# A spectral filter and a gated feed-forward in one kernel: the first block's filter sums, weight conversions, GpSimd sums and two copies are moved

## The chip, the cores and the metric

The kernel runs on one core of one Trainium2 chip. The metric is the device time of one execution in microseconds (us); lower is better. Each engine of the core (TensorE, here PE; VectorE, DVE; ScalarE, ACT; GpSimd, POOL; SyncE, SP) works through its own instructions in the order in which the program issues them, and waits on semaphores for the others. Transfers are issued by SP, ACT or POOL and run on 16 DMA engines.

## The reference

```python
# x: (8, 3008, 256); filt_r, filt_i: (1505, 256); w_in: (256, 2048); w_out: (2048, 256)
X = np.fft.rfft(x, axis=1)
y = np.fft.irfft(X * (filt_r + 1j * filt_i)[None], n=3008, axis=1)   # a filter along the sequence
t = y.reshape(24064, 256)
h = t @ w_in
g = h * np.clip(h + 3.0, 0.0, 6.0) / 6.0
out = g @ w_out
```

Everything is float32 in the result. The kernel may be handed weights whose words the program has to reassemble (`w_conv` below), so each piece of `w_in` and `w_out` passes through a "conversion" before it can be used.

## The kernel before, in words

**The two halves.** The first half turns each of the 8 batches into its spectrum, multiplies by the filter and turns it back. The length 3008 is split as 47 times 64, so the transform is a product with small tables (`a_unit`, L385), a second product (`b_unit`), the filter (`f_unit`, L449 to L451, and its sums in `y_unit`, L459 and L460), a first product back (`bi_unit`, L471 with its copies L474) and a last one (`n_unit`, L524), which writes the tokens into a ring in SBUF (`xn`). Between these steps the data goes through DRAM: `z_store` and `t2_load`, `g_store` and `t4_load`.

The second half takes 512 tokens at a time (a "block", 47 of them) and for each block walks through 8 pieces `p` of the hidden dimension, 256 wide each. One (block, piece) pair is a **step**; steps are numbered 0, 1, 2, ... over all blocks. Block 0 (steps 0 to 7) uses plain products: `plain_up(p)` (L657, 8 instructions on PE), `relu` on ACT (L615), `hswish` on DVE (L620), and one step later `plain_down(p)` (L668, 16 instructions). From block 1 on, a Strassen-like scheme with 7 instead of 8 products is used (`up_1` to `up_5`, L570; `down`, L646). It needs sums of quarter matrices: of the tokens (`t_sums`, POOL, L563), and of the weights (`w_sums`, POOL, L299), the latter made once for all blocks.

**Conversions.** The 16 weight pieces, `w_in[0]`, `w_out[0]`, `w_in[1]`, ..., `w_out[7]`, are numbered 0 to 15. Number i is loaded by SP (`w_load`, L260), has its absolute value taken by ACT (`w_abs`, L266) and is finished by seven DVE instructions (L275, L277, L279, L281, L288, L290, L293), which write it into `w_all`. The staging buffers are few, so the load of a later piece is issued only behind the conversion that frees its buffer; the read that frees it is L288. Numbers 0 to 3 are converted before step 0 ends its first products; the other 12 are put into the steps by a list. Converted piece 2p is needed by `plain_up(p)` at step p, piece 2p+1 by `plain_down(p)` at step p+1.

**Order.** [...] `at(step, fn, ...)` puts a piece of work of the first half, of the conversions or of the sums into a step. In a step of block 0 the order is `plain_up(p)`, then the work put there that PE should meet early (`a_unit`, `b_unit`, `bi_unit`, `n_unit`), then `plain_down(p-1)`, then the rest in the order in which it was put there. An engine's instruction that has to wait holds up all that the program put behind it on that engine.

**Buffers that the change touches.** `rp` has two buffers, used by `relu` and, in batch 0, also for the two results of `y_unit` (i = 10 and 11, made just before step 0). Their last readers are the matmuls of `bi_unit(0, 10)` at step 0, which the program issues behind `plain_up(0)`; the two `relu` of step 0 therefore wait for them. `t1p` has two buffers too. Batch 0 uses them for the results of `bi_unit(0, 0)`, `(0, 4)` and `(0, 8)` on their way to DRAM; from step 2 on, `a_unit` of batch 1 uses them. The PSUM banks of `plain_up` (`al`, `be`) are single: the products of step p+1 wait until `hswish` of step p has read them.

**Batch 1.** Its `a_unit(1, c)`, c = 0 to 7, lies in steps 2 to 9, one a step. Each has two 128x512 results in PSUM, which ACT copies to SBUF (L388), and four stores on SP (`z_store`, L402).

Of the kernel before, what the change touches and what calls it, by code (L numbers as in the profile page):

```python
# [10 lines left out]
FP32 = mybir.dt.float32  # L11
# [20 lines left out]
P = 128  # L32
D = 256
# [5 lines left out]
NB = HC // XC  # L39
# [6 lines left out]
NP = DFF // 256  # L46
# [90 lines left out]
def kernel(  # L137
# [9 lines left out]
    nc = tc.nc  # L147
# [15 lines left out]
    def pool(name, bufs, **kw):  # L163
        return ctx.enter_context(tc.tile_pool(name=name, bufs=bufs, **kw))

    const = pool("const", 1)
    t1p = pool("t1p", 2)
    t2p = pool("t2p", TB)
    sp = pool("sp", 2)
    yp = pool("yp", 3)  # L170
    t3p = pool("t3p", T3B)
    xtp = pool("xtp", 2)
    rp = pool("rp", 2)
# [21 lines left out]
    st = {}  # L195
# [173 lines left out]
    def bank(b):  # L369
        if b:  # L370
            return psF.tile([P, 512], FP32, name="psf", tag="f")
        st["bank"] = i = (st.get("bank", -1) + 1) % 4
        return psO.tile([P, 2, 2, P], FP32, name="po%d" % i).rearrange("p a u m -> p (a u m)")
# [4 lines left out]
    def a_unit(b, c):  # L378
        xc = xs[:, (b * NB + c) % 3, :, :]
        t = t1p.tile([P, XC // 2, 2, D], FP32, name="t1")  # L380
        ps = [bank(b).rearrange("p (j d) -> p j d", d=D) for h in range(2)]
        for j in range(2):
            for g in range(2):
                for h in range(2):
                    nc.tensor.matmul(ps[h][ts(g, 64), j, :], wa[ds(h * 64, NA), ds((c * XC + 2 * g + j) * 2 * KH, 64)],  # L385
                                     xc[ds(h * 64, NA), 2 * g + j, :], start=True, stop=True)
        for h in range(2 if b == 1 else 1):
            nc.scalar.activation(out=t[:, :, h, :], in_=ps[h], func=AXT.Copy)  # L388
        st["t1", b, c] = t, ps[1]


    def a_sums(b, c):
        t, ps = st["t1", b, c]
        nc.vector.tensor_tensor(out=t[:, :, 1, :], in0=t[:, :, 0, :], in1=ps, op=ALU.subtract)
        nc.vector.tensor_tensor(out=t[:, :, 0, :], in0=t[:, :, 0, :], in1=ps, op=ALU.add)  # L395

# [56 lines left out]

    def y_unit(b, i):
        s1, s2 = st["y", b, i]
        y = yp.tile([P, 2, D], FP32, name="y") if b else rp.tile([P, 512], FP32, name="r", tag="r").rearrange(
            "p (u d) -> p u d", u=2)
        re, im = slice(0, HALF), slice(HALF, P)
        nc.vector.tensor_tensor(out=y[re], in0=s1[re], in1=s1[im], op=ALU.subtract)  # L459
        nc.vector.tensor_tensor(out=y[im], in0=s2[re], in1=s2[im], op=ALU.add)  # L460
        st["y", b, i] = y
# [34 lines left out]
    for b in range(B):  # L496
        j = 0
        while j < HC:
            n = 1 if b == 0 and j == NJ else min(NJ, HC - j)
# [229 lines left out]


    EARLY = (a_unit, b_unit, bi_unit, n_unit)

    def at(step, fn, *a):
        plan.setdefault((step, fn in EARLY), []).append((fn, a))

    with tc.manual_schedule():
# [38 lines left out]
        ps = psU.tile([P, 512], FP32, name="al")  # L775
# [27 lines left out]
        for c in range(NT):  # L803
            for i in (2 * c, 2 * c + 1):
                b_unit(0, i)
                f_unit(0, i)
                if c == NT - 1:
                    y_unit(0, i)
            if c + 1 < NT:
                turn(c + 1)  # L810
            if c:
                bi_unit(0, 2 * c - 2)
                (g0_first if c == NT - 1 else lambda i: g_store(0, i))(2 * c - 2)
            if c == 4:
                t4_load(0, 0, KH - 3 * TC, 1)
# [20 lines left out]
        at(0, bi_unit, 0, NU - 2)  # L836
        at(0, g_store, 0, NU - 2)

        for i, s in enumerate((0, 1, 1, 2, 2, 3, 3, 4, 4, 5, 5, 6)):
            at(s, convert_one)  # L840
        for p in range(NP):
            for i in range(2):
                for late in range(2):
                    at(p + 6, w_sums, 2 * p + i, late)

        at(0, wai_load)
        at(2, x_load, 1, 2)
# [31 lines left out]
        def places(n):  # L879
            if n == 1:  # L880
                return (list(range(2, NB + 2)), [12, 13, 15, 18, 19, 20, 22, 23, 26, 27, 28, 30],
                        [14, 15, 16, 19, 21, 22, 24, 25, 27, 29, 30, 31], [16, 21, 24, 29, 31, 32])
            k = first[n] * NP
            a_at = [k - 7 * NP + i for i in (2, 4, 7, 9, 11, 13, 14, 15)]
            f_at, y_at, bi_at = ([k - (5 - 2 * r) * NP + i for r in range(2) for i in p]
                                 for p in ((2, 3, 6, 7, 12, 13), (4, 5, 10, 11, 14, 15), (8, 14, 17)))
            return a_at, f_at, y_at, bi_at

        prev = None
        for n in range(1, B):  # L890
            a_at, f_at, y_at, bi_at = places(n)
            for c, s in enumerate(a_at):
                at(s, a_unit, n, c)
                if n > 1:
                    at(s, a_sums, n, c)
                at(s, z_store, n, c, nc.sync if n == 1 else nc.gpsimd)
                if c >= 3:
                    at(max(a_at[c - 3], s - 6), x_load, n, c)
                elif n > 1:
                    at(max(prev[c + NB - 3], s - 6), x_load, n, c)  # L900
            for c in range(NT):
                s = f_at[2 * (c - TB) + (n == 1)] + 1 if c >= TB else a_at[-1] + 1
                at(s, t2_load, n, c)
                s = f_at[2 * (c - FB) + 1] + 1 if c >= FB else a_at[-1 if n > 1 else 3] + 1
                at(s, table_load, n, c)
            for i in range(NU):
                if i % 2 == 0 or n == 1:
                    at(f_at[i], b_unit, n, i)
                if i % 2 == 0:
                    at(bi_at[i // 2], bi_unit, n, i)  # L910
                    at(bi_at[i // 2], g_store, n, i)
                at(y_at[i], y_unit, n, i)
            for i in range(NU):
                at(f_at[i], f_unit, n, i)
            prev = a_at
# [4 lines left out]
        for i in range(len(items) + 1):  # L920
            up = i < len(items)
            k, p = items[min(i, len(items) - 1)]
# [92 lines left out]
```

## Time and profile before

| | |
|---|---|
| median of 4 runs | 2708.49 us (2707.42 to 2710.55) |
| the profiled execution | 2706.81 us; span from first to last instruction 2705.0 us |
| busy in the span | PE 2677.1 us, DVE 2024.2, ACT 1308.0, POOL 374.0 |
| step 0 starts on PE (first L657) | 67.48 us |
| step 8 (block 1) starts on PE | 140.70 us |
| PE busy from 66 to 142 us | 68.74 of 76 us |
| DVE busy from 66 to 142 us | 66.97 of 76 us |

How to read it: "busy" is the time in which an engine runs an instruction. The chain that ended last is followed back from the last instruction to what released each step. In the timeline, a number in brackets is how long the engine sat idle before the instruction, and what ended that. L-numbers are lines of the kernel before.

### The profile page before, as it was taken

What the parts mean: (1) busy time and instruction counts of PE and PEld (TensorE: products, weight loads), DVE (VectorE), ACT (ScalarE), POOL (GpSimd) and SP (SyncE); (2) the same over time, 40 slices, a digit from 0 to 9 for tenths busy, and PEclk for the clock granted to TensorE, in tenths of its full rate; (3) what the DMA queues carried; (4) which work ended last, traced back from release to release, by engine and by line L of the source; (5) the groups of instructions that cost most, each with busy time, mean ns of one, the idle gap of its engine ahead of it and who ended that gap; (6) DMA issues with size and microseconds to landing.
All of it is one profiled execution on the core that took longest, in us unless ns stands there. A gap on an engine that the chain in (4) does not pass through costs nothing.

```text
span 2705.0 us, 48891 instructions
## 1 busy us (share of the span) xinstructions
PE 2677.1 (99%) x18846; PEld 2366.4 (87%) x18846; DVE 2024.2 (75%) x3503; ACT 1308.0 (48%) x2614; POOL 374.0 (14%) x598
## 2 busy tenths in 40 slices
PE   8899999999999999999999999999999999999998
PEld 6588888888988889888888888988888888899997
DVE  7968867787677876787767877678776778766665
ACT  3344444445544454444454545445445454445443
POOL 2421111100110011100121011210112111000000
PEclk9999999999999999999999999999999999999999
DMA  9632133211232113311133111331113321110000
GB/s 236 205 104 72 45 82 103 74 33 41 83 105 69 35 41 92 101 63 36 46 98 96 55 39 51 91 96 55 38 55 88 95 58 37 42 31 18 18 9 17
DMA packets 106598, 185.89 MB, mean 69 GB/s; under 512 B 23609, under 2 KB 66297, under 8 KB 106049
## 3 DMA queue, kind: packets, MB, share of 16 engines
q1 hardware_dynamic: 88607, 138.05, 17.8%
q0 software_dynamic: 17152, 44.22, 6.2%
q8 instruction: 149, 2.44, 0.4%
q14 instruction: 84, 0.69, 0.1%
q10 hardware_dynamic: 606, 0.49, 0.1%
HBM read 110.74 MB, written 71.93 MB: 68 GB/s over the span
## 4 chain that ended last, share of the span: by engine, by line
PE 96%; DVE 3%; DMA 1%; issue 0%; ACT 0%; SPq 0%; POOL 0%; POOLq 0%; DVEq 0%
PE po L646 43%; PE al L570 24%; PE be L570 18%; PE psn L524 4%; PE psf L471 2%; PE psf L385 2%; PE psf L428 1%; PE po L352 1%; PE po L437 0%; PE psf L437 0%; DVE g L620 0%; DVE y L277 0%; DVE y L288 0%; DVE y L290 0%; DVE w_all L293 0%; PE al L779 0%
## 5 line engine op out<-in xcount | busy, mean ns | idle before, releaser
L646 PEld LDWEIGHTS po<-w_all,g 128*128 128x128 f32 x10304 | 1363.2, 191 | 149.5 <-issue 41.4
L646 PE MATMUL po<-w_all,g 128*128 128x128 f32 x10304 | 1403.3, 276 | 0.6 <-DVE g L620 0.6
L615 ACT ACTIVATE r<-h,half_c 128x512 f32<-128x512 f32 x736 | 531.3, 722 | 329.5 <-DVE h L596 317.5
L620 DVE SCALAR_TENSOR_TENSOR g<-r,h 128x512 f32<-128x512 f32 x736 | 507.6, 690 | 206.8 <-ACT r L615 193.0
L570 PE MATMUL al<-xt,w_all 128*128 128x256 f32 x2208 | 660.1, 381 | 1.2 <-DVE h L601 0.6
L570 PE MATMUL be<-xn,w_all 128*128 128x256 f32 x1472 | 437.8, 379 | 0.0
L596 DVE TENSOR_TENSOR h<-be,s 128x512 f32<-128x512 f32 x368 | 254.3, 691 | 220.6 <-PE be L570 209.8
L570 PEld LDWEIGHTS al<-xt,w_all 128*128 128x128 f32 x2208 | 335.3, 192 | 2.5 <-issue 1.3
L570 PEld LDWEIGHTS be<-xn,w_all 128*128 128x128 f32 x1472 | 279.7, 190 | 37.9
L610 ACT ACTIVATE h<-al 128x256 f32<-128x256 f32 x368 | 141.4, 384 | 343.1 <-PE al L570 343.1
L601 DVE TENSOR_TENSOR h<-al,s 128x256 f32<-128x256 f32 x368 | 156.3, 425 | 165.8 <-PE al L570 164.8
L628 DVE TENSOR_TENSOR g<-g 128x512 f32<-128x512 f32 x368 | 255.9, 695 | 12.6
L591 ACT ACTIVATE s<-al 128x256 f32<-128x256 f32 x368 | 141.4, 384 | 205.5 <-PE al L570 203.3
L582 ACT ACTIVATE s<-be 128x256 f32<-128x256 f32 x368 | 141.4, 384 | 176.3 <-PE be L570 176.3
L570 PE MATMUL al<-xn,w_all 128*128 128x256 f32 x736 | 219.9, 381 | 0.5 <-ACT h L610 0.5
L570 PE MATMUL be<-xt,w_all 128*128 128x256 f32 x736 | 218.9, 379 | 0.0
L630 DVE TENSOR_TENSOR g<-g 128x256 f32<-128x256 f32 x368 | 169.8, 462 | 12.5
L581 ACT ACTIVATE s<-al 128x256 f32<-128x256 f32 x368 | 141.4, 384 | 70.8 <-PE al L570 70.8
L627 DVE TENSOR_TENSOR g<-g 128x256 f32<-128x256 f32 x368 | 157.1, 427 | 12.6
L570 PEld LDWEIGHTS be<-xt,w_all 128*128 128x128 f32 x736 | 139.8, 190 | 18.9
L402 POOL DMA_DIRECT2D z_tmp<-t x192 | 95.6, 505 | 417.2 <-DVE t L395 398.8
L563 POOL TENSOR_TENSOR xt<-xn 128x256 f32<-128x256 f32 x92 | 68.7, 746 | 471.9 <-ACT xn L530 451.7
(139 smaller groups left out, 1810.9 us busy)
## 6 DMA issues: line engine op xcount, KB each, us to landing
g_tmp<-t POOLq DMA_DIRECT2D x96, 256.0 KB, 3.7
t<-g_tmp SPq DMA_DIRECT2D x188, 120.0 KB
t<-z_tmp SPq DMA_DIRECT2D x42, 512.0 KB
z_tmp<-t POOLq DMA_DIRECT2D x192, 96.0 KB, 3.1
out_dram<-o SPq DMA_DIRECT2D x321, 47.0 KB
xs<-in_x_dram SPq DMA_DIRECT2D x112, 128.0 KB
ft<-in_filt_r_dram SPq DMA_DIRECT2D x168, 64.0 KB
ft<-in_filt_i_dram SPq DMA_DIRECT2D x168, 64.0 KB
```

The lines of the kernel that those rows point to most:

```text
L570: nc.tensor.matmul(ps, w_in[p][:, w, :], x, start=start, stop=stop, skip_group_check=True)
L581: nc.scalar.activation(out=s[:, 0, :], in_=al, func=AXT.Copy)
L582: nc.scalar.activation(out=s5, in_=be[:, 1, :], func=AXT.Copy)
L591: nc.scalar.activation(out=s[:, 1, :], in_=al, func=AXT.Copy)
L596: nc.vector.tensor_tensor(out=st["h"][0].rearrange("p (a n) -> p a n", a=2), in0=be, in1=s, op=ALU.add)
L601: nc.vector.tensor_tensor(out=st["h"][1][:, 256:512], in0=al, in1=s5, op=ALU.add)
L615: nc.scalar.activation(out=r, in_=st["h"][i], func=AXT.Relu, bias=half_c, scale=1.0 / 6.0)
L620: nc.vector.scalar_tensor_tensor(out=st["g", k, p][:, o:o + 2, :].rearrange("p a n -> p (a n)"), in0=st["r", i], scalar=1.0, in1=st["h"][i ...
L627: v.tensor_tensor(out=g[:, G1, :], in0=g[:, G3, :], in1=g[:, G22, :], op=ALU.add)
L628: v.tensor_tensor(out=g[:, G3:G2 + 1:2, :], in0=g[:, G3:G1 + 1, :], in1=g[:, G11:G11 + 1, :].broadcast_to([P, 2, 256]), op=ALU.subtract)
L630: v.tensor_tensor(out=g[:, G4, :], in0=g[:, G12, :], in1=g[:, G2, :], op=ALU.subtract)
L646: nc.tensor.matmul(st["po", k][bank][:, part, u, :], g[:, a, ts(u, P)], w_out[p][:, w, :], start=(p == 0 and n in OPENS and u == 0), stop= ...
```

## The change

Four edits, all in the work around steps 0 to 13:

1. `y_unit` of batch 0 writes both results into one buffer of `t1p` and no longer into the two of `rp`. It takes that buffer between `bi_unit(0, 4)` and `bi_unit(0, 8)`, so that the latter, and all later users of `t1p`, get the other one of the two.
2. The 12 listed conversions go to steps 0,0,1,2,2,3,4,4,5,5,6,7 and no longer to 0,1,1,2,2,3,3,4,4,5,5,6. Numbers 5, 10, 12, 14 and 15 change their step; 5 comes a step earlier, the others a step later.
3. The first three sums of piece 14 (`w_in[7]`) are issued as the first `w_sums` of all, at step 6 behind conversion 14, which they read; all other sums stand behind them on POOL. The fourth sum of piece 14 comes last, at step 13.
4. For c = 6 and 7 of batch 1 (steps 8 and 9) the second of the two copies goes from ACT to DVE, at the end of the step.

```diff
-        for h in range(2 if b == 1 else 1):
+        for h in range(2 if b == 1 and c < NB - 2 else 1):
             nc.scalar.activation(out=t[:, :, h, :], in_=ps[h], func=AXT.Copy)
...
     def a_sums(b, c):
         t, ps = st["t1", b, c]
+        if b == 1:
+            if c >= NB - 2:
+                nc.vector.tensor_copy(out=t[:, :, 1, :], in_=ps)
+            return
...
     def y_unit(b, i):
         s1, s2 = st["y", b, i]
-        y = yp.tile([P, 2, D], FP32, name="y") if b else rp.tile([P, 512], FP32, name="r", tag="r").rearrange(
-            "p (u d) -> p u d", u=2)
+        if b == 0 and i % 2 == 0:
+            st["y0"] = t1p.tile([P, 2, 2, D], FP32, name="t1")
+        y = yp.tile([P, 2, D], FP32, name="y") if b else st["y0"][:, i % 2, :, :]
...
-        for i, s in enumerate((0, 1, 1, 2, 2, 3, 3, 4, 4, 5, 5, 6)):
+        for i, s in enumerate((0, 0, 1, 2, 2, 3, 4, 4, 5, 5, 6, 7)):
             at(s, convert_one)
-        for p in range(NP):
-            for i in range(2):
-                for late in range(2):
-                    at(p + 6, w_sums, 2 * p + i, late)
+
+        order = [2 * NP - 2] + [i for i in range(2 * NP) if i != 2 * NP - 2]
+        for i in order:
+            at((6 + i // 2) if i != order[0] else 6, w_sums, i, False)
+            if i != order[0]:
+                at(6 + i // 2, w_sums, i, True)
+        at(6 + NP - 1, w_sums, order[0], True)
...
             for c, s in enumerate(a_at):
                 at(s, a_unit, n, c)
-                if n > 1:
-                    at(s, a_sums, n, c)
+                at(s, a_sums, n, c)
```

## The prediction

> **What bounds the kernel now.** I read the page first, then the engines' waits between 66 and 142 us (block 0), then the timeline there and around the first `bi_unit`s. Page, busy time by engine and the chain's shares; then the waits of PE and POOL in 66 to 142 us; then a table of stretches:
>
> ```profile
> PE 2677.1 (99%) x18846; PEld 2366.4 (87%) x18846; DVE 2024.2 (75%) x3503; ACT 1308.0 (48%) x2614; POOL 374.0 (14%) x598
> PE 96%; DVE 3%; DMA 1%; issue 0%; ACT 0%; SPq 0%; POOL 0%; POOLq 0%; DVEq 0%
> ...
> PE al L657 <- DVE g L620: 6.8, 4, 3.0
> ...
> POOL xt L563 <- DVE y L288: 20.2, 1, 20.2
> ...
> 118.00:120.00 2.00, 0.01 (x1) 0.00 (x0) 1.86 (x3) 0.00 (x0) 1.84 (x4) 1.00 0.09 18
> 122.00:124.00 2.00, 2.00 (x4) 0.86 (x3) 1.95 (x3) 0.70 (x2) 1.92 (x4) 0.56 0.87 308
> ```
>
> PE bounds all but the start. The change lies where PE is not the bound: in block 0 it waits for DVE (6.8 us in 4 waits), and after the longest wait its granted clock fell to 0.56, so that one `plain_up` took 5.3 us and not 3.5 (hidden: DVE was later still). So the question is when DVE reaches the last `hswish` that PE waits for. From 132.49 us, when step 7 starts, PE is dense. Lines of the timeline that carry the sums:
>
> ```profile
> 52.42 0.60 ACT L474 ACTIVATE t<-psf 128x512 f32<-128x512 f32 x1 [2.34 <-PE psf L471]
> 72.28 0.69 ACT L615 ACTIVATE r<-al,half_c 128x512 f32<-128x512 f32 x1 [4.12 <-PE psf L471]
> 73.00 0.69 DVE L620 SCALAR_TENSOR_TENSOR g<-r,al 128x512 f32<-128x512 f32 x1 [2.65 <-DMA xs<-in_x_dram]
> ...
> 106.68 28.46 POOL L299 TENSOR_TENSOR w_all<-w_all 128x128 f32<-128x128 f32 x40
> 121.05 2.63 PE L657 MATMUL al<-xn,w_all 128*128 128x512 f32 x4 [3.03 <-DVE g L620]
> 132.49 1.99 PE L657 MATMUL al<-xn,w_all 128*128 128x512 f32 x4 [1.37 <-DVE g L620]
> 144.25 0.39 ACT L591 ACTIVATE s<-al 128x256 f32<-128x256 f32 x1
> 144.79 0.67 PE L570 MATMUL al<-xt,w_all 128*128 128x256 f32 x2 [0.55 <-ACT s L591]
> ```
>
> Seen here: the first `relu` waits for `bi_unit` (L471), though its product was done at 69.4; behind it DVE stands 2.65 us. (The "DMA xs" there is only the last semaphore; ACT's wait names the cause.) 40 weight sums run on POOL just while DVE converts. With POOL idle a conversion takes 4.18 us (79.58 to 83.75), beside the sums 4.97, 5.24, 4.98 and 5.27 (numbers 11 to 14, from their first lines).
>
> **Part by part.** Durations are from the profiled execution, whose own time is 2706.81 us; that is 1.7 below the median of the four, so I work out a difference and subtract it from the median.
>
> *y in `t1p`.* Same DVE instructions. `relu` then waits only for its products: 67.48 + 1.95 = 69.4 and, for the second, be's end 71.2. `hswish` runs when conversion 3 ends (70.35) and at 71.95; DVE is free at 72.55 and not at 74.20: 1.65 us. PE goes on at 72.1, behind `bi_unit`. The price: `bi_unit(0, 8)` takes the buffer of `bi_unit(0, 4)`, whose two stores POOL issued at 45.7 and 46.3; they landed 5.6 and 6.2 us later, at up to 52.5, and ACT's copy starts at 52.42. The chain of the start runs through the second copy at 53.28, which waits for PE anyway. So 0 as measured; the slowest store of this stretch took 9.0 us to land, which would cost 2.6. I take 0, the row of this very transfer.
>
> *Sums behind conversion 14.* Numbers 11 to 14 lose 0.79 + 1.06 + 0.80 + 1.09 = 3.7 us, and number 10 about 0.2. What stays is `t_sums(1)`: 0.34 on number 8 (its last instruction 1.03, not 0.69) and some 1.3 on number 10 (5.73 - 4.18, less the weight sums' part). I take the rows. The Trainium skill (page "SBUF — State Buffer", section "Who interferes with whom") says that a DVE instruction with two SBUF inputs and a GpSimd instruction that reads SBUF block each other whole, whichever starts second. By that rule alone much of the 28.46 us of sums would be DVE's loss, and the gain several times larger.
>
> What is queued behind the new wait on POOL: all other sums and the second `t_sums`. Conversion 14 will end at about 129.3; three sums at 0.71 (28.46/40) to 131.4, four of `w_in[0]` to 134.3, needed at step 8's start, 137.6: hidden with 3.3 us to spare. After that POOL makes 8 sums in 5.7 us per step of 7.3, and `t_sums(2)` waited for tokens until 168.6 anyhow. The sums now run beside steps 7 to 12. From 172 to 186 us 24 of them ran beside such steps with PE busy without a gap: cost 0. The bounds: 0, or all that DVE loses, 0.66 us a step there (0.93, 0.56, 0.83 and 0.56 against 0.69, 0.42, 0.69 and 0.42) for 4.2 steps, 2.8 us.
>
> *Conversions spread.* The same 12, but PE now waits for some of them: `plain_up(5)`, `(6)`, `(7)` need numbers 10, 12, 14, which end one step before. Step by step; U is the start of `plain_up`, H of `hswish`. PE's step lasts 8.1 us (80.73 to 88.84), 9.9 with an `n_unit` (88.84 to 98.75). H is DVE's free time, but at least U + 2.65, and U + 4.36 for its second half (98.75; 100.67 + 0.69; 102.38 + 0.69). The pair takes 1.2, and U is at least H + 0.74.
>
> - Step 0: 4 and 5 end at 72.55 + 2 x 4.18 = 80.9. H(1) = 80.9 (before 78.39), U(2) = 81.65 (80.73). PE, done at 79.2, stands 2.45 us.
> - 6 ends at 86.3, H(2) there; 7 and 8 end at 96.2. U(3) = 89.8, U(4) = 99.7: PE sets them. H(3) = 96.2, 9 ends at 101.55.
> - H(4) = 102.3 and 104.0: DVE waits 1.9 us for PE. 10, beside `t_sums(1)`, takes 5.5: 110.15. U(5) = 110.2 (109.64). 11 ends at 114.35.
> - H(5) = 114.35; 12 ends at 119.75, U(6) = 119.8 (121.05); 13 at 123.9, H(6) there, 14 at 129.3.
> - U(7) = 129.35 (132.49), U(8) = 129.35 + 8.2 = 137.6 (140.70): 3.1 us gained.
>
> Number 15 then lies beside PE's dense step 7: H(7) ends at 134.5, it takes up to 5.3, done at 139.8; `plain_down(7)` needs it at U(8) + 4.6 = 142.2, and the next DVE work (L596) at 141.5. Cover 1.7 us.
>
> On SP the loads move along. Load 9 now waits for number 5's L288 (79.5) ahead of the tables for `n_unit` and `t4_load`, which started at 77.45 and now at 80: 2 us later, for a use 1.0 us later (93.3 for 92.27). Between 0 and 1.2; I take 0, as `n_unit` didn't wait at all. Loads 12, 13 and 14 go out behind the L288 of 10, 11 and 12, at 107.8, 113.0, 118.4, and have 7.8, 6.8 and 6.8 us; landings before took 3.7 to 5.7 us (107.33 to 111.7 the first). Hidden by 1.1 at least. Load 15 moves to 122.5, and behind it on SP are `z_store(1, 3)` and `x_load(1, 6)`; they end by 131, needed at 139.
>
> *Two copies on DVE.* At step 8 ACT makes one copy (0.6) and not two (1.08) before L591, which starts 0.4 us earlier; PE's 0.55 shrinks: 0.4 gained. On DVE the copy, 0.69 by the same shape's row, falls into gaps of 3.75 us (step 8) and 1.47 (step 9). The stores that need them stand behind 14 output stores on SP until 160: hidden. At step 9 nothing is gained, L591 is not awaited.
>
> Sum: 3.1 + 0.4 = 3.5 us, 0.13%. 2708.5 - 3.5 = **2705.0 us** (the profiled execution about 2703.3). From U(8) on all is PE-bound and shifts.
>
> **The rivals.**
> - *More is gained.* If DVE's 1.9 us of standing and `t_sums`' 1.6 go away, PE's own step times bind: 72.1 + 7.1 + 8.1 + 9.9 + 9.9 + 3 x 8.1 = 131.4 for U(8), a gain of 9.3 + 0.4: 2698.8 at best. Faster by over 0.2% needs 5.4. For it: PE has 6.8 us of waits. Against: `plain_up(5)` to `(7)` start the moment a conversion ends.
> - *The clock gate makes it slower.* PE gets three gaps, 2.45, 1.5 and 1.4 us, before steps 2, 6 and 7. A gap of 3.03 us brought 0.56, one of 1.54 at 72.2 nothing. Each lowered clock costs 5.3 - 3.5 = 1.8 us. In step 2 it goes through in full (gain 1.7 left); in step 6 it delays H(6)'s second half by 1.45, in step 7 again 1.8: 5.05 in all, 1.5 us slower than before, 2710.0. It needs at least two of the three. The Trainium skill (page "TensorE: Matmul & The Clock Gate", section "What's actually happening") has the clock fall after an idle window of about 3.4 us; by that rule none of the three gaps trips it and the sum stays 3.5, but the gap of 3.03 us in this trace, shorter than that window, did.
> - *The change doesn't do what it says in edit 1.* If dependencies are kept for whole tiles, the matmuls that read the first y (54.23) wait for the second (57.7): 3.5 us, of which 1.4 hide behind `n_first`'s load: gain 1.4, 2707.1. Against: at 27.57 PE reads half of a tile whose other half DVE finishes at 28.04.
> - *The loads bind.* Each us by which loads 12 and 14 land later than 7.8 and 6.8 us is lost; at 9.1 us the gain is gone (1.3 + 2.3): 2708.5.
>
> **How the numbers follow.** 0.2% (5.4 us) is about what a measurement of this kernel tells from no change. Forecast with its small terms 0.5 (2703 to 2707); more gained 0.27, nearly all of it over 0.2%; clock gate 0.09, whole tiles 0.04, loads 0.05; the rest, 0.05, something unnamed, slower. That puts 0.27 on faster, 0.63 on same; slower by over 0.2% takes a mishap larger than any I can price, or several, 0.10. The range goes from the dense PE (2699.0) to the clock rival: 2709.5.
>
> **What would show it.** The first `relu` at 69.4 with no wait on L471; no L299 before conversion 14's last L293; conversions 11 to 14 at 4.2 us; U(2) about a us later than before, U(7) and U(8) about 3 us earlier; L591 of step 8 not behind two L388. Wrong: a lowered clock in steps 2, 6 or 7; w_abs waiting for loads with DVE standing; PE waiting on L299 at step 8; `bi_unit(0, 8)`'s copy waiting for a store.

## The result and the profile after

The changed kernel takes 2704.83 us (median of 42 executions, 2702.86 to 2708.69), the kernel before 2708.21 us (60 executions beside it): the ratio is 0.9987, 95% interval 0.9983 to 0.9992. That is 3.4 us or 0.13% less; 3.5 us and 2705.0 us were predicted. The profiled execution took 2702.86 us, span 2701.1.

The page of the changed kernel, busy time by engine and the shares of the chain, and then the waits of PE and of POOL from 66 to 142 us (who waited for whom: us in total, times, longest). In this kernel's numbering `plain_up` is L662, `hswish` L625, `relu` L620, the copies of `bi_unit` L479, the Strassen products L575; L596 is the L591 of before:

```profile
PE 2675.5 (99%) x18846; PEld 2365.7 (88%) x18846; DVE 2022.9 (75%) x3505; ACT 1305.2 (48%) x2612; POOL 367.1 (14%) x598
PE 97%; DVE 2%; DMA 0%; ACT 0%; issue 0%; POOL 0%; SPq 0%; POOLq 0%; DVEq 0%
...
PE al L662 <- DVE w_all L293: 3.0, 3, 1.2
PE al L662 <- DVE g L625: 2.4, 1, 2.4
...
POOL w_all L299 <- issue: 21.8, 1, 21.8
```

The page hardly moves: 3.4 us are too little for it. The waits do. PE no longer waits four times for `hswish` (6.8 us before) but once, and three times for the last instruction of a conversion, 5.4 us in all. POOL stands 21.8 us; the releaser is not named there, but the timeline shows its first sum start 0.13 us after conversion 14's last instruction ends. The lines of the timeline that answer to those of before:

```profile
52.56 1.29 ACT L479 ACTIVATE t<-psf 128x512 f32<-128x512 f32 x2 [2.50 <-DMA g_tmp<-t]
67.37 1.98 PE L662 MATMUL al<-xn,w_all 128*128 128x512 f32 x4 [0.34 <-ACT xn L559]
69.39 0.69 ACT L620 ACTIVATE r<-al,half_c 128x512 f32<-128x512 f32 x1 [1.37 <-PE al L662]
71.83 0.69 DVE L625 SCALAR_TENSOR_TENSOR g<-r,be 128x512 f32<-128x512 f32 x1 [0.77 <-ACT r L620]
81.52 1.98 PE L662 MATMUL al<-xn,w_all 128*128 128x512 f32 x4 [2.35 <-DVE g L625]
...
125.17 0.42 DVE L275 TENSOR_SCALAR y<-bits 128x512 int32<-128x512 int32 x1
...
128.77 0.69 DVE L293 SCALAR_TENSOR_TENSOR w_all<-s,y 128x512 f32<-128x512 f32 x1
129.51 1.98 PE L662 MATMUL al<-xn,w_all 128*128 128x512 f32 x4 [1.19 <-DVE w_all L293]
129.59 24.14 POOL L299 TENSOR_TENSOR w_all<-w_all 128x128 f32<-128x128 f32 x43 [21.79 <-issue]
137.73 0.59 PE L575 MATMUL al<-xn,w_all 128*128 128x256 f32 x2
...
140.87 0.38 ACT L596 ACTIVATE s<-al 128x256 f32<-128x256 f32 x1
141.40 0.67 PE L575 MATMUL al<-xt,w_all 128*128 128x256 f32 x2
```

The first `relu` (L620) starts at 69.39, as soon as its product is there, and not at 72.28. Conversion 14 ends at 129.46 (128.77 + 0.69); `plain_up(7)` starts 0.05 us after that and the sums 0.13. In step 8, L575 no longer has 0.55 us of waiting in front of it. The first line shows the price of edit 1: the copy of `bi_unit(0, 8)` now waits for a store out of its buffer, and starts at 52.56 and not at 52.42; the stores of `bi_unit(0, 8)` still go out at 53.88 (53.90 before) and step 0 still starts at 67.37 (67.48 before), so it costs nothing.

### The profile page after: what moved, and what is told of

Read it like the earlier page. It is cut to its first block, busy times and chain, and to the rows that moved or that the text cites. A ratio compares the mean times of both kernels' runs of the same rounds, so it can differ in the third digit from the quotient of the medians.

```text
span 2701.1 us, 48889 instructions
## 1 busy us (share of the span) xinstructions
PE 2675.5 (99%) x18846; PEld 2365.7 (88%) x18846; DVE 2022.9 (75%) x3505; ACT 1305.2 (48%) x2612; POOL 367.1 (14%) x598
## 4 chain that ended last, share of the span: by engine, by line
PE 97%; DVE 2%; DMA 0%; ACT 0%; issue 0%; POOL 0%; SPq 0%; POOLq 0%; DVEq 0%
PE po L651 43%; PE al L575 24%; PE be L575 18%; PE psn L529 4%; PE psf L476 2%; PE psf L385 2%; PE psf L432 1%; PE po L352 1%; PE po L673 1%; PE po L441 0%; PE psf L441 0%; PE al L662 0%; PE be L662 0%; PE al L784 0%; DMA g_tmp<-t 0%; DVE g L625 0%
## 5 line engine op out<-in xcount | busy, mean ns | idle before, releaser
L620 ACT ACTIVATE r<-h,half_c 128x512 f32<-128x512 f32 x736 | 531.0, 721 | 329.4 <-DVE h L601 317.3
L625 DVE SCALAR_TENSOR_TENSOR g<-r,h 128x512 f32<-128x512 f32 x736 | 508.4, 691 | 205.1 <-ACT r L620 190.3
L575 PE MATMUL al<-xt,w_all 128*128 128x256 f32 x2208 | 660.1, 381 | 0.8 <-DVE h L606 0.6
L575 PE MATMUL be<-xn,w_all 128*128 128x256 f32 x1472 | 437.8, 379 | 0.0
L575 PEld LDWEIGHTS al<-xt,w_all 128*128 128x128 f32 x2208 | 335.3, 192 | 2.1 <-DVE h L606 1.2
L575 PEld LDWEIGHTS be<-xn,w_all 128*128 128x128 f32 x1472 | 279.7, 190 | 37.9
L596 ACT ACTIVATE s<-al 128x256 f32<-128x256 f32 x368 | 141.2, 384 | 206.2 <-PE al L575 204.1
L575 PE MATMUL al<-xn,w_all 128*128 128x256 f32 x736 | 219.9, 381 | 0.5 <-ACT h L615 0.5
L575 PE MATMUL be<-xt,w_all 128*128 128x256 f32 x736 | 218.9, 379 | 0.0
L575 PEld LDWEIGHTS be<-xt,w_all 128*128 128x128 f32 x736 | 139.8, 190 | 18.9
L496 POOL DMA_DIRECT2D g_tmp<-t x84 | 52.7, 632 | 582.7 <-ACT t L479 582.7
```

Source lines behind the costliest of these rows:

```text
L575: nc.tensor.matmul(ps, w_in[p][:, w, :], x, start=start, stop=stop, skip_group_check=True)
L596: nc.scalar.activation(out=s[:, 1, :], in_=al, func=AXT.Copy)
L620: nc.scalar.activation(out=r, in_=st["h"][i], func=AXT.Relu, bias=half_c, scale=1.0 / 6.0)
L625: nc.vector.scalar_tensor_tensor(out=st["g", k, p][:, o:o + 2, :].rearrange("p a n -> p (a n)"), in0=st["r", i], scalar=1.0, in1=st["h"][i ...
```

## The experiments

Edits 1 to 3 tell between the start of step 0 on PE and that of step 8, edit 4 in step 8 itself, and behind that PE has hardly a gap; so beside the medians each profile gives one number that does not depend on where the execution began: **start of step 8 less start of step 0**. It is 140.70 - 67.48 = 73.22 us for the kernel before and 137.73 - 67.37 = 70.36 us for the changed one. It leaves edit 4 out. All results in one table (medians of 5 to 11 executions, of the changed kernel 42 and of the kernel before 60; "lowered clock" are the steps of block 0 in which the granted clock fell in that profile, "hidden" where PE's next step waited for DVE longer anyway; line numbers differ by up to six between the kernels):

| kernel | median, us | before beside it | ratio (95%) | step 8 - step 0 | lowered clock |
|---|---|---|---|---|---|
| before | 2708.21 | | | 73.22 | step 6 (hidden) |
| changed | 2704.83 | 2708.21 | 0.9987 (0.9983 to 0.9992) | 70.36 | none |
| changed, again | 2704.92 | 2707.60 | 0.9988 (0.9979 to 0.9997) | 72.04 | step 2 |
| without edit 1 | 2706.50 | 2708.47 | 0.9992 (0.9983 to 1.0001) | 73.70 | step 2 |
| without edit 2 | 2700.65 | 2708.47 | 0.9972 (0.9960 to 0.9984) | 67.70 | none |
| without edit 2, again | 2701.03 | 2707.60 | 0.9976 (0.9967 to 0.9984) | 67.70 | none |
| without edit 3 | 2710.21 | 2708.47 | 1.0005 (0.9997 to 1.0014) | 76.55 | steps 6 (hidden but for 0.2 us), 7 |
| without edit 4 | 2705.76 | 2708.47 | 0.9991 (0.9982 to 1.0000) | 70.35 | none |
| edit 1 alone | 2705.55 | 2708.70 | 0.9990 (0.9981 to 0.9999) | 71.57 | step 6 (hidden) |
| edit 2 alone | 2713.38 | 2708.70 | 1.0016 (1.0007 to 1.0025) | 81.57 | steps 0, 2, 7 |
| edit 3 alone | 2703.04 | 2708.70 | 0.9979 (0.9971 to 0.9988) | 69.35 | none |
| swapped | 2698.69 | 2708.70 | 0.9963 (0.9951 to 0.9976) | 64.73 | none |
| swapped, again | 2698.50 | 2707.60 | 0.9968 (0.9955 to 0.9980) | 64.73 | none |
| gap filled | 2703.66 | 2708.26 | 0.9988 (0.9979 to 0.9997) | 70.35 | none |

**The edits one at a time, off the changed kernel.** Edit 1 undone:

```diff
-        if b == 0 and i % 2 == 0:
-            st["y0"] = t1p.tile([P, 2, 2, D], FP32, name="t1")
-        y = yp.tile([P, 2, D], FP32, name="y") if b else st["y0"][:, i % 2, :, :]
+        y = yp.tile([P, 2, D], FP32, name="y") if b else rp.tile([P, 512], FP32, name="r", tag="r").rearrange(
+            "p (u d) -> p u d", u=2)
```

> The changed kernel with edit 1 undone: the two results of y_unit again in relu's buffers, all else as changed. My theory: DVE's chain in block 0 sets the start of step 7, and PE's waits in steps 2 to 4 hang on that same chain, so the 1.65 us go through whole: 1.7 us slower than the changed kernel, 1.8 us faster than the kernel before (2706.5), the first relu again waits 4 us for bi_unit, step 2 starts at 83.2 and step 8 at 139.3. Rival: DVE stands 1.9 us at step 4 anyway and swallows the shift; then the time is that of the changed kernel (2704.8).

Measured 2706.50 us, 1.7 above the changed kernel's first median. Its profile, the waits of ACT from 66 to 80 us, and the windows of 2 us in which step 2 lies (busy us of PE, PEld, DVE, ACT and POOL with counts, then the granted clock, DMA share and GB/s):

```profile
ACT r L619 <- PE psf L475: 4.2, 1, 4.2
...
84.00:86.00 2.00, 2.00 (x3) 0.66 (x2) 1.90 (x6) 0.00 (x0) 0.00 (x0) 0.50 1.12 431
86.00:88.00 2.00, 2.00 (x5) 0.85 (x4) 1.86 (x3) 0.69 (x1) 0.00 (x0) 0.77 0.99 411
```

The wait for `bi_unit` is back, 4.2 us. Step 2 starts at 83.49 (83.2 expected). But then this execution lost more than the theory says: after its 2.40 us gap PE ran the start of step 2 at 0.50 and then 0.77 of its clock, and the step took 9.90 us and not the 8.22 of the changed kernel (89.74 - 81.52). Taking these 1.68 off 73.70 leaves 72.02, 1.66 more than 70.36: the 1.65 of the prediction. The rival, that DVE's standing at step 4 swallows it, falls.

Edit 2 undone, the older places of the conversions:

```diff
-        for i, s in enumerate((0, 0, 1, 2, 2, 3, 4, 4, 5, 5, 6, 7)):
+        for i, s in enumerate((0, 1, 1, 2, 2, 3, 3, 4, 4, 5, 5, 6)):
```

> The changed kernel with edit 2 undone: conversions at steps 0,1,1,2,2,3,3,4,4,5,5,6, all else as changed. My theory: the spreading is the one part that costs, as plain_up(5), (6) and (7) wait for conversions that end one step before, and DVE stands at step 4; undone, step 2 starts at 79.2, step 7 at 126.9 and step 8 at 135.1 instead of 137.7: 2.5 us faster than the changed kernel, 5.9 us faster than before (2702.3). Rival: the spreading pays, since loads and conversions no longer crowd; then 1 to 4 us slower than the changed kernel (2706 to 2709), with w_abs waiting for loads.

> The changed kernel with edit 2 undone, once more. By the starts of step 8 in the profiles (137.73 and 135.13) it is 2.6 us faster than the changed kernel; by the medians of different chip jobs 4.2. If the order of DVE is all there is, 2.6; if something outside block 0 gains too, about 4.

Both profiles have 67.70: 2.66 us less than the changed kernel, with step 7 at 126.92 and step 8 at 135.13 in the first, as expected to 0.03. Its waits of PE from 60 to 160 us, those of DVE up to 140, and the lines of its timeline where steps 0, 7 and 8 start:

```profile
PE al L662 <- DVE g L625: 3.0, 3, 1.3
...
DVE h L601 <- PE be L575: 5.1, 1, 5.1
DVE g L625 <- ACT r L620: 0.7, 1, 0.7
...
67.43 1.98 PE L662 MATMUL al<-xn,w_all 128*128 128x512 f32 x4 [0.34 <-ACT xn L559]
126.92 1.98 PE L662 MATMUL al<-xn,w_all 128*128 128x512 f32 x4 [1.27 <-DVE g L625]
135.13 0.59 PE L575 MATMUL al<-xn,w_all 128*128 128x256 f32 x2
```

PE's 2.4 us before step 2 are gone. DVE stands 0.7 us for `relu`, at step 0; the changed kernel's timeline has 0.77 there, 1.14 and 1.03 at step 4, and 2.79 and 1.03 at step 7. (The 5.1 us lie at step 8, where DVE has nothing left to do.) No `w_abs` holds up DVE. So the spreading costs, and the rival that it pays falls. The medians lie 3.9 us apart on the same chip (2704.92 and 2701.03): 1.2 more than 2.66. Nothing outside block 0 gains: from the start of step 8 to the end both profiles of that chip take 2563.4 us (2703.2 - 139.81 and 2699.3 - 135.90). The rest is put down to the clock behind the gap before step 2, which this kernel doesn't have; filling that gap, below, brings as much.

Edit 3 undone, GpSimd's sums where they were:

```diff
-        order = [2 * NP - 2] + [i for i in range(2 * NP) if i != 2 * NP - 2]
-        for i in order:
-            at((6 + i // 2) if i != order[0] else 6, w_sums, i, False)
-            if i != order[0]:
-                at(6 + i // 2, w_sums, i, True)
-        at(6 + NP - 1, w_sums, order[0], True)
+        for p in range(NP):
+            for i in range(2):
+                for late in range(2):
+                    at(p + 6, w_sums, 2 * p + i, late)
```

> The changed kernel with edit 3 undone: GpSimd's sums start as soon as their pieces are converted, all else as changed. My theory: conversions 11 to 14 take 5.0 to 5.3 us again instead of 4.2, and every one of them lies on the chain, so 3.9 us slower than the changed kernel and 0.5 us slower than before (2708.7); step 8 starts near 141.5. Rival: PE's step times bind before DVE does, and half of it or less is lost (2706.8 or less). Rival by a full lock-out of VectorE while a sum runs: 8 us or more (2713).

Measured 2710.21, 5.4 above the changed kernel. Lines of its timeline, conversion 14 and the step behind it:

```profile
129.15 0.66 DVE L275 TENSOR_SCALAR y<-bits 128x512 int32<-128x512 int32 x1
129.84 0.83 DVE L277 SCALAR_TENSOR_TENSOR y<-bits,top_c,y 128x512 int32<-128x512 int32 x1
130.70 0.56 DVE L279 TENSOR_SCALAR y<-y 128x512 int32<-128x512 int32 x1
131.18 0.68 DVE L281 TENSOR_SCALAR bits<-bits 128x512 int32<-128x512 int32 x1
...
133.72 0.73 DVE L293 SCALAR_TENSOR_TENSOR w_all<-s,y 128x512 f32<-128x512 f32 x1
134.50 2.52 PE L662 MATMUL al<-xn,w_all 128*128 128x512 f32 x4 [2.04 <-DVE w_all L293]
136.81 3.09 PE L662 MATMUL be<-xn,w_all 128*128 128x512 f32 x4
```

Conversion 14 takes 129.15 to 134.45, 5.30 us, where it takes 4.29 in the changed kernel (125.17 to 129.46). Numbers 10 to 13 lose 0.4, 1.1, 0.8 and 1.1 in the same way, together 4.3 us. Step 7 starts at 134.50, less 67.86 for the start 66.64, against 62.14: 4.5 us; the other 0.2 is the second `hswish` of step 6, late behind that step's lowered clock. On top, PE's gap of 2.04 us brought a lowered clock in step 7 (9.91 us and not 8.22), which is the rest of the 6.2 us between 76.55 and 70.36. Half of it hidden, or 8 us lost by a full lock-out, the two rivals, both fall.

Edit 4 undone:

```diff
-        for h in range(2 if b == 1 and c < NB - 2 else 1):
+        for h in range(2 if b == 1 else 1):
...
         if b == 1:
-            if c >= NB - 2:
-                nc.vector.tensor_copy(out=t[:, :, 1, :], in_=ps)
             return
```

> The changed kernel with edit 4 undone: ACT makes both copies of batch 1's last two a_units, all else as changed. My theory: L596 of step 8 stands behind the second copy and PE waits 0.5 us there: 0.4 us slower than the changed kernel (2705.2). Rival: nothing (2704.8), as ACT's wait is taken up by PE's next wait in step 9 (0.5 us for L615).

By the medians 0.8 to 0.9 us slower, which the intervals don't settle. The profile does, in its timeline at step 8 (which starts at 138.19):

```profile
140.77 1.08 ACT L388 ACTIVATE t<-psf 128x512 f32<-128x512 f32 x2 [0.70 <-PE psf L385]
141.74 0.39 ACT L594 ACTIVATE s<-al 128x256 f32<-128x256 f32 x1
142.28 0.67 PE L573 MATMUL al<-xt,w_all 128*128 128x256 f32 x2 [0.54 <-ACT s L594]
```

The two copies are back on ACT and PE waits 0.54 us: 142.28 - 138.19 = 4.09 us from the start of step 8, against 141.40 - 137.73 = 3.67: 0.42 us, the 0.4 expected. It is not taken up in step 9, as the rival has it: PE's second `n_unit` behind step 8 starts 26.32 us after that step's start (164.51 - 138.19), in the changed kernel 25.91 (163.64 - 137.73).

**The edits alone, on the kernel before** (the same lines as above, the other way round).

> The kernel before with edit 1 alone. My theory: DVE is the bound from step 0 to step 7, so 1.65 us less there is 1.65 us less at the end: 2706.6. Rival: PE's waits move with it and the gain is lost at steps 2 to 4 (2708.2), or the later user of the store's buffer delays the first tokens by up to 2.6 us (2709).

71.57, that is 1.65 us less than 73.22, to the hundredth. The median is 3.1 us below the kernel before; the interval of the ratio (0.3 to 5.1 us) holds both. In the profile neither rival shows.

> The kernel before with edit 3 alone (sums behind conversion 14, which is in step 5 there). My theory: conversions 10 to 14 take 4.2 us, 3.9 us less on a chain where DVE is the bound throughout: 2704.3, as fast as the whole change. Rival: the sums come late for step 8 or slow steps 7 to 12, and 1 to 3 us of it are lost again (2705 to 2707).

69.35: 3.87 us less than 73.22, and 1.0 less than the whole change; the median is 2703.04 us. Conversions 11 to 14 take 4.2 to 4.3 us; number 10, beside the sums of the tokens (`t_sums`), still takes 5.53. Nothing of it is lost in steps 7 to 12: from the start of step 8 to the end it is 2564.2 us (2701.2 - 137.02), and 2564.3 before.

> The kernel before with edit 2 alone (the spread conversions). My theory: with the sums still beside them, conversions 12 and 14 end just before plain_up(6) and (7) needs them: step 7 starts near 134.9 instead of 132.5, so 2.4 us slower, 2710.6; PE stands about 3 us before step 6, where its clock may fall, hidden behind DVE. Rival: the spreading pays by itself, 1 to 3 us faster (2705 to 2707).

Slower, 2713.38 us, by 4.7 and not by 2.4. The profiled execution (2716.37, one of the slowest of the 11) has these waits of PE from 66 to 152 us, and these products of step 7 in its timeline:

```profile
PE al L657 <- DVE w_all L293: 7.1, 3, 3.0
PE al L657 <- DVE g L620: 3.9, 2, 2.4
...
140.71 2.89 PE L657 MATMUL al<-xn,w_all 128*128 128x512 f32 x4 [3.02 <-DVE w_all L293]
143.40 2.71 PE L657 MATMUL be<-xn,w_all 128*128 128x512 f32 x4
```

PE waits 11.0 us and its clock fell in steps 0, 2 and 7. Steps 0, 2 and 7 took 8.40, 9.91 and 9.91 us, against 6.26, 8.11 and 8.21 in the kernel before: some 5.6 us that the 81.57 holds. Without them it is about 75.9, 2.7 more than before, and the fastest of the 11 executions, 2710.19, is near the 2710.6 expected. Why the clock also fell at step 0, behind a gap of 1.43 us only (1.39 in the kernel before, where it didn't), stays open; that place is ahead of anything edit 2 moves.

Put together, edits 1 and 3, each measured alone, add up without a remainder: 73.22 - 1.65 - 3.87 = 67.70, which is what the kernel without edit 2 has. Edit 2 adds 2.66 to that, measured off the changed kernel; alone it adds about as much (2.7), but only once its lowered clocks are taken out.

**The clock.** The same changed kernel gave 70.36 and 72.04 in two executions.

> The changed kernel itself once more, beside the next two on the same chip: 3.4 us faster than the kernel before, as in its first runs; PE starts step 8 at 137.7.

The second profile's windows from 82 us, and the first one's for the same windows:

```profile
82.00:84.00 2.00, 2.00 (x3) 0.88 (x4) 1.93 (x5) 0.00 (x0) 0.00 (x0) 0.61 1.08 433
84.00:86.00 2.00, 2.00 (x4) 0.82 (x3) 1.83 (x5) 0.69 (x1) 0.00 (x0) 0.54 1.06 447
```

```profile
82.00:84.00 2.00, 2.00 (x6) 0.95 (x5) 1.92 (x5) 0.46 (x1) 0.00 (x0) 1.00 1.12 415
84.00:86.00 2.00, 2.00 (x19) 0.70 (x17) 1.84 (x3) 0.92 (x2) 0.00 (x0) 1.00 1.00 370
```

PE is busy throughout in both, but with 0.61 and 0.54 of its clock it gets to 7 instructions in the second execution and to 25 in the first. The gap before it is 2.34 us in the one and 2.35 in the other. The step takes 9.91 us (91.82 - 81.91) and not 8.22, and step 8 comes 1.68 us later. To see what this costs on the whole, the gap was filled:

```diff
+        def warm(n):
+            ps = psF.tile([P, 512], FP32, name="psf", tag="f")
+            for i in range(n):
+                nc.tensor.matmul(ps[0:TOK, :], wai[:, 0, :], xn[:, 0, 0:512], start=True, stop=True)
+
+        at(1, warm, 2)
```

> The changed kernel with two extra products of 128x512 on PE at the end of step 1, whose result nobody reads, so that PE's gap before step 2 shrinks from 2.35 to about 0.6 us. In two profiles of the changed kernel the same gap (2.35 and 2.34) left the clock whole once and lowered it once, at 1.7 us. My theory: with the gap filled the clock never falls in step 2, step 8 starts 70.4 us after step 0 (as in the first profile, not 72.0 as in the second), and the median falls by the share of executions in which it had fallen, 0.5 to 1.7 us (2703.2 to 2704.4). Rival: the spread between executions has another cause, and the median stays at 2704.9.

The two extra products (each counts as two instructions) and the start of step 2 in its timeline:

```profile
79.01 1.88 PE L857 MATMUL psf<-xn,wai 128*94 128x512 f32 x4
81.52 1.98 PE L662 MATMUL al<-xn,w_all 128*128 128x512 f32 x4 [0.63 <-DVE g L625]
```

The gap is 0.63 us, step 8 comes 70.35 us after step 0, and the median is 2703.66, 1.2 lower than the changed kernel's. Of the first 42 executions of the changed kernel 12 lie below 2704.0 and 25 between 2704.0 and 2705.5; with the gap filled it is 7 of 11 below 2704.0 and none in the second stretch. So the rival, that the spread between executions has another cause, falls for this part of it; that the 25 are those in which the clock fell is read from their times, as only two executions of the changed kernel have a profile (2702.86 us without the fall, 2704.97 with it). Five and four lie at 2706.6 and above; the filled gap does not touch those, and their cause stays open.

**A better order.** If DVE's order alone sets block 0, then a piece that `plain_up` needs at a step's start should be converted ahead of one that `plain_down` needs a step later:

```diff
     def w_part(i):
+        i = {11: 12, 12: 11, 13: 14, 14: 13}.get(i, i)
         p = i // 2
...
-        for i, s in enumerate((0, 0, 1, 2, 2, 3, 4, 4, 5, 5, 6, 7)):
+        for i, s in enumerate((0, 1, 1, 2, 2, 3, 3, 4, 5, 5, 6, 7)):
...
-        order = [2 * NP - 2] + [i for i in range(2 * NP) if i != 2 * NP - 2]
+        order = [2 * NP - 3] + [i for i in range(2 * NP) if i != 2 * NP - 3]
```

> The changed kernel with another order of conversions: pieces 11 and 12, and 13 and 14, change places (w_in[6] before w_out[5], w_in[7] before w_out[6]), the steps are 0,1,1,2,2,3,3,4,5,5,6,7, and the three sums that hold up POOL are those of w_out[6]. If DVE's order is what sets block 0, then the piece that plain_up needs comes before the one that is needed a step later, PE runs dense from step 2 on, step 7 starts at 123.3 and step 8 at 131.4: 6.3 us faster than the changed kernel, 2698.5. If the loads or SP bind once DVE no longer does, it stays at 2701 to 2705.

> The kernel with the swapped conversions, once more: by the starts of step 8, 132.99 with a first step that began 0.9 us later, 5.6 us faster than the changed kernel, and 2.1 to 3 us faster than the one with edit 2 undone.

64.73 both times, 5.63 us less than the changed kernel, and 2698.5 to 2698.7 us: 9.1 and 10.0 us faster than the kernel before beside it. The waits of PE from 60 to 160 us in the first of the two, and the lines where steps 0 and 8 start:

```profile
PE psn L558 <- DMA xs<-in_x_dram: 2.0, 1, 2.0
PE al L663 <- DVE g L626: 0.6, 1, 0.6
PE al L576 <- ACT h L616: 0.5, 1, 0.5
PE al L663 <- ACT xn L560: 0.3, 1, 0.3
...
68.26 1.98 PE L663 MATMUL al<-xn,w_all 128*128 128x512 f32 x4 [0.34 <-ACT xn L560]
132.99 0.59 PE L576 MATMUL al<-xn,w_all 128*128 128x256 f32 x2
```

Of the 5.4 us that PE waited for DVE in block 0, 0.6 are left, before step 5; so the gain is 5.63 and not the 6.3 expected of a dense PE. The loads don't bind. The run changes two things at once: it also moves the first eight listed conversions back to where they were before edit 2. The kernel without edit 2 gains 2.66 of the 5.63; the other 2.97 come with the swapped pairs and the later places of the last four, which no run takes apart.

## Why the prediction was right

| start on PE, us | predicted | measured |
|---|---|---|
| U(2) | 81.65 | 81.52 |
| U(3), U(4) | 89.8, 99.7 | 89.74, 99.65 |
| U(5) | 110.2 | 110.40 |
| U(6) | 119.8 | 119.95 |
| U(7) | 129.35 | 129.51 |
| U(8) | 137.6 | 137.73 |

Step 0 began 0.11 us earlier here than in the rows that the prediction used. Counted from it, U(2) to U(4) are met to 0.06 us, and U(5) to U(8) come 0.24 to 0.31 later than predicted; about half of that is number 10, which beside `t_sums` took 5.65 us and not 5.5. So block 0 gained 2.86 us and not 3.1.

- **y in `t1p`**: 1.65 us predicted, 1.65 alone and 1.66 off the changed kernel. The wait for the store was there, 0.14 us, and hidden behind the second copy, as reckoned. Whole-tile dependencies, the third rival, did not show: PE reads the first y from 54.20 us (54.23 before), while DVE writes the second from 56.28 on.
- **Sums behind conversion 14**: 3.9 us predicted; 3.87 alone, 4.5 off the changed kernel, where numbers 10, 11 and 13 lost more than the rows of before said (0.4, 1.1 and 1.1 for 0.2, 0.8 and 0.8), number 12 less (0.8 for 1.1), and 0.2 came with the lowered clock in step 6. The rule of the Trainium skill (page "SBUF — State Buffer", section "Who interferes with whom"), that the loser blocks whole, would by the prediction's estimate have made the gain several times larger; the runs bear out the rows.
- **Conversions spread**: the cost stood in the prediction only as waits inside the recurrence, never as a term with a sign. It is +2.66 us. The prediction had all it takes to see that this edit takes back nearly half of what the others bring (1.65 + 3.87 + 0.42), and did not draw it.
- **POOL, steps 7 to 12**: 0 taken, 2.8 as the bound; 0 measured (edit 3 alone: 8.21 us for step 7 and 2564.2 behind it, 8.21 and 2564.3 before).
- **SP**: loads 9 and 12 to 15 were hidden, as taken; `n_unit` did not wait.
- **Two copies**: 0.4 predicted, 0.42 measured.
- **The clock** was the misjudged term. It was a rival at 0.09, told as a way to end slower. By the times of its executions it belongs to the changed kernel's common execution, in the first of the three steps named and at the size given (1.8 predicted, 1.68 measured), but it does not decide the sign. The gaps of 1.17 and 1.19 us before steps 6 and 7 never tripped it.

So the mechanism was right, but that the medians meet the forecast to 0.1 us (3.4 for 3.5) is in part luck. Block 0 and edit 4 gave 2.86 + 0.42 = 3.28 us, and the clock's fall, which the sum put at nothing, takes some 1.2 of it in the median, by the filled gap. Against it stands that the median of the kernel before lies 1.4 us above the execution that was profiled (2708.21 and 2706.81), and no run shows why. The two profiled executions, both without the clock's fall in step 2, lie 3.95 us apart (2706.81 and 2702.86); 0.1 of the rest is the earlier start of step 0, and 0.6 is in none of the terms.

## What to carry to other kernels

When two engines take turns, write the start of every step as the latest of its releasers, with durations from the rows; here this held to 0.3 us over 70 us, and it tells for each part of a change whether it pays, so evaluate it once for each part by itself. Convert what the next step's start needs before what its end needs: the swapped order, with the first eight conversions back in their older places, brought 5.63 us in block 0 on top of the 2.86 of the change. A gap on PE costs more than its length when the clock falls behind it (1.7 us here), so a gap ahead of a stretch in which PE is the bound is worth filling; one behind which PE waits for DVE anyway cost nothing in two kernels and 0.2 us in a third.

## What the runs showed of the hardware that was not expected

- The granted clock fell behind shorter gaps than the 3.03 us of the kernel before, and not each time. Gaps of 2.34 to 2.40 us before step 2 brought it down in 3 of 6 profiles, gaps of 3.02 to 3.04 before steps 6 and 7 in 4 of 5, one of 2.04 did so once; gaps of 0.6 to 1.4 before steps 5 to 7 and of 1.54 before step 1 never did, one of 1.43 ahead of step 0 did once. The Trainium skill (page "TensorE: Matmul & The Clock Gate", section "What's actually happening") gives an idle window of about 3.4 us; no gap here was that long, so the measurement decides.
- Beside GpSimd's sums, DVE's one-input instructions lose more than the two-input ones. The kernel before, groups of DVE instructions by line from 74 to 96 us (POOL idle), then from 110 to 131 us (sums running); after the count: busy us, mean ns of one:

```profile
L288 DVE SCALAR_TENSOR_TENSOR y<-bits,y 128x512 f32<-128x512 f32 x2 | 1.4, 692 | 0.1
L281 DVE TENSOR_SCALAR bits<-bits 128x512 int32<-128x512 int32 x2 | 0.8, 422 | 0.0
...
L288 DVE SCALAR_TENSOR_TENSOR y<-bits,y 128x512 f32<-128x512 f32 x4 | 3.3, 826 | 0.1
L281 DVE TENSOR_SCALAR bits<-bits 128x512 int32<-128x512 int32 x4 | 2.7, 679 | 0.0
```

  692 to 826 ns for two inputs, 422 to 679 for one.
